# Later reciprocals, later queue issues and three more VectorE groups in a planned kernel of attention and a gated feed-forward part

## The chip, the cores and the metric

The kernel runs on one core of one Trainium2 chip. A core has five engines that run side by side, each through its own list of instructions in order: TensorE (PE, matrix products), ScalarE (ACT), VectorE (DVE), GpSimd (POOL) and SyncE (SP), which here only issues DMA transfers. TensorE writes to PSUM, eight banks of 128 x 512 fp32; the other data lie in SBUF. The metric is the device time of one execution in microseconds (us); several runs are given by their median.

## The reference

With x of 2048 x 512 (bfloat16), 32 heads of 16, and a hidden width of 1792:

```python
xn = _layernorm(x, axis=-1)
# A: attention
qkv = (xn @ wqkv).reshape(B, S, 3, H, Dh)          # q, k, v: 32 heads x 2048 x 16
scores = einsum("bhqd,bhkd->bhqk", q, k) * (Dh ** -0.5)
p = softmax(scores, axis=-1)
o = einsum("bhqk,bhkd->bhqd", p, v)
# B: gated feed-forward
gate, up = xn @ W_gate, xn @ W_up
h = gate * (gate > 0) * up
out = x + o.reshape(B, S, D) @ wo + h @ W_down
```

There are 32 x 2048 x 2048 exponentials, 134 million of them. They are the bulk of the elementwise work.

## The kernel before

**Tiling.** The queries are cut into four chunks of 512 (`c4`), the heads into four groups (`gg`) of eight, and each group into its even and odd heads (`ee`): 32 blocks of four heads, in that order. The keys of a block are 16 tiles of 128 (`kt`). For one block and one key tile the scores of four heads are four tiles of 128 x 512. They are turned into exponentials in one of two ways.

- *ScalarE's way.* Two units for a key tile (`p` = 0, 1), each of two heads: TensorE writes scores into two PSUM banks (`P_sc` holds two such pairs), ScalarE makes one `Exp` of 128 x 1024 into a ring of 16 buffers (line 1347), and TensorE multiplies the tile by the values once.
- *VectorE's way, a group* (`quad`). The scores go one head at a time into one of the four shared banks (`P_b`). VectorE evicts each with an added bias into a 16-bit integer whose bits, read as bfloat16, are a rough exponential (line 1300). Two more patterns are made by adding a constant to all of these integers: the first by GpSimd or VectorE, by the share `POOL1_SHARE`, the second always by GpSimd, each in two pieces (line 1316; on VectorE line 1320, one instruction). The last two groups have both on VectorE (`LASTD`). TensorE multiplies all three by the values and adds them up, three value products where the other way has one; together they approximate the exponential.

`QUADS` says how many key tiles of each of the 32 blocks go VectorE's way (149 of 512 in all, so 1024 - 2 x 149 = 726 units are ScalarE's), and `QOFF` and, in the last block, `LAST_QUADS` say at which tiles: `int((a + QOFF) * 16 / q)` for a = 0 ... q - 1.

**Matmul form.** A matmul uses 64 rows and 32 columns of the array. Four of them side by side fill a half, and the two halves run independently (`mode="half"`). Weights are loaded by separate instructions; a load is left out when the half already holds the same ones (`wkey`), as between the three value products of a group when they follow each other.

**Sums.** The value matrix has a column of ones, so the softmax sums come out as one row of each head's product. When a block's products are complete, `normalise` (from line 1168) evicts the accumulator into `o_sb` (L1178), copies the sums into `rsum` by a DMA spread over 128 partitions (L1194), has VectorE take 128 x 16 reciprocals (L1198), stores these in DRAM (L1199), loads them back broadcast (L1202), and has GpSimd multiply (L1210 or L1215); for odd heads four DMAs then pack the result (`pk`, L1219).

**Background.** Projections of queries, keys and values, and 56 feed-forward tiles (`glu`: two weight loads L980 and L981 into three buffers, two products, evictions L989 and L993) and 16 output row tiles (`out_rows`) run on TensorE and VectorE between the scores, at due times counted in ScalarE units. `K_LEAD`, `Q_LEAD`, `W_LEAD`, `V_AT` and `WREST` are leads or places in such units. A projected query goes through `qf` and eight small DMAs (L873) to its four masked copies.

**The planner.** All operations are put into a `Graph` with reads, writes, duration and priority. `Graph.run` simulates the engines and fixes the order of instructions on each; `Graph.emit` adds the semaphore waits. In `ready(o)` an operation may start at the planned end of what it reads, plus its `slack` where the producer is neither TensorE nor a DMA; after a DMA, `DMA_SLACK` = 1000 ns later, or at once where that DMA is marked urgent, as the sums' copies of the last blocks are. A buffer that is not yet given is taken from the moment when its last user ends. These times set the order alone; on the chip an engine waits for the semaphore, and whatever stands behind the waiting instruction on that engine or queue waits too. `slot_for` gives out the four shared banks: accumulators (`open`) hold a bank for a whole block, and the last block has two of them (`LAST2`), the second with `extra` set. `TOGETHER = 2` puts all three value products of a group behind the second pattern in the order. The two lines that the change touches in `ready` are

```python
at = max(at, d.end if d.eng == "PE" else d.end + ((0.0 if d.urgent else self.DMA_SLACK) if d.eng == "SP" else o.slack))
...
    at = max(at, b[0])
```

Of the kernel before, what the change touches and what calls it, by code (L numbers as in the profile page):

```python
# [32 lines left out]
PV_SLACK = 100  # L33
W_LEAD = 12
Q_LEAD = 36
K_LEAD = 28
QN, KN, GN, RN = 3, 2, 5, 10
ROW_AT = 16
XBANKS = (0, 1, 2, 3)
# [3 lines left out]
NRAW = 4  # L43
NPAT = 5
LEAD = 15
QOFF = 0.2
EARLY = ()
AHEAD = 10
POOL_SHARE = 1.0
POOL_PIECES = 2  # L50
POOL1_SHARE = 0.5
TOGETHER = 2
LAST2 = 1
LASTD = 2
TAIL_URGENT = 3
SC_ORDER = (0, 2, 1, 3)
P1_OFF = 0.0
LAST_QUADS = 0.8
SPLIT = 8
PVBANKS = (0, 1, 2, 3)  # L60
PV_EARLY = False
REC = 'DVE'
POOL_NS = 1980
QUADS = [0, 3, 4, 4, 5, 5, 5, 5, 5, 5, 5, 5, 5, 4, 5, 5, 5, 5, 5, 5, 5, 5, 5, 4, 5, 5, 5, 5, 5, 5, 5, 5]


LOG2E = 1.4426950408889634
# [5 lines left out]
TR_URGENT = (0, 1, 1, 1)  # L73
TR_AFTER = (None, 1, None, None)
DMA_TR = (2, 3)
WREST = 6
Z_AT = 20
MASK_ACT = (0, 2)
MASK_LATE = 4
PER_TILE = (0,)  # L80
V_AT = (4, 8, 14, 20)
EXP_SCALE = 1.0 / (128.0 * LOG2E)
NUP = 1
NHS = 20
# [36 lines left out]
class Graph:  # L121
# [16 lines left out]

    def __init__(self):
        self.ops = []  # L140
        self.fillers, self.nfill = [], 0
        self.units = {}

    def op(self, eng, dur, fn, reads=(), writes=(), prio=0.0, order=(), name="", stream=None, lat=None, after=None,
# [44 lines left out]
    def run(self):  # L189
# [18 lines left out]
        def slot_for(t):  # L208

            best, second = None, None  # L210
            for i in (t.allowed if t.allowed is not None else range(len(t.pool.cur))):
                c = t.pool.cur[i]
                if c is None:
                    at = 0.0
                else:
                    us = c.w + c.r
                    if not all(u.done for u in us):
                        continue
                    at = max(u.end for u in us)
                if best is None or at < best[0]:  # L220
                    best, second = (at, i), best
                elif second is None or at < second[0]:
                    second = (at, i)
            if t.pool.shared:
                held = any(c is not None and c.open > 0 for c in t.pool.cur)
                if t.extra:
                    if t.extra.slot is None:
                        return None
                elif t.open:
                    if held and not (self.EARLY and second is not None):  # L230
                        return None
                elif not held and len(t.allowed) > 3:
                    return second
            return best

# [4 lines left out]
        def ready(o):  # L240
            at = 0.0
            for d in o.deps:
                at = max(at, d.end if d.eng == "PE" else d.end + ((0.0 if d.urgent else self.DMA_SLACK) if d.eng == "SP" else o.slack))
            for d in o.order:
                at = max(at, d.start if d.eng == o.eng else d.end)
            for t in o.acq:
                if t.slot is not None:
                    continue
                b = slot_for(t)
                if b is None:  # L250
                    return None
                at = max(at, b[0])
            return at

        def pe_start(o, at):
# [10 lines left out]
        held = [None, None]  # L266
# [53 lines left out]
        while n < len(ops):  # L320
# [8 lines left out]
            if got_pe is not None and best[1] == "PE":  # L329
                at, o = got_pe  # L330
                kind = None
                for f in self.fillers:
                    t = f[0].cur[f[1]]
# [25 lines left out]
            at, e, o = best  # L359
# [208 lines left out]
def bass_parallel_sum__mha_block__glu_gated_reglu__prompt_kernel(  # L568
# [14 lines left out]
    with ExitStack() as es:  # L583
        def sb(name, shape, dt):
# [34 lines left out]
        rsum = sb("rsum", [128, 2, 16], FP32)  # L619
        rrec = sb("rrec", [128, 2, 16], FP32)  # L620
# [8 lines left out]
        G = Graph()  # L629
# [25 lines left out]
             reads=[t_pid], writes=[t_pid], prio=-890)  # L655
        for v in (0, 2, 1, 3):
            G.op("DVE", 100, lambda e, v=v: e.tensor_scalar(hmask[:, v:v + 1], pid[:, 0:1], 16.0 * v, QSCALE, op0=ALU.is_equal, op1=ALU.mult),
                 reads=[t_pid], writes=[t_masks[v]], prio=-889 + v)
# [4 lines left out]
             reads=[t_id], writes=[t_id], prio=-898)  # L663
# [8 lines left out]

        def dma(fn, kb, writes=(), reads=(), prio=0.0, stream=None, order=(), name="dma", after=None, joins=()):
            return G.op("SP", 500, fn, reads=reads, writes=writes, prio=prio, stream=stream or ("o", len(G.ops)),
                        lat=kb, order=order, name=name, after=after, joins=joins)

        x_src = x2.rearrange("(m p) d -> p m d", p=128)
        t_x = [Tile("x") for _ in range(NB)]
# [42 lines left out]
        for j in range(4):  # L721
            for ee in range(2):
                r0 = 32 * j + DH * ee
                dma(lambda e, r0=r0, ee=ee: e.dma_start(Wo_l[r0:r0 + DH, ee, :], A_wo[D - 128 + r0:D - 128 + r0 + DH, :]), 16,
                    reads=[t_woz], writes=[Tile()], prio=60, after=100)
# [178 lines left out]
        for n, bk in enumerate(blocks):  # L904
            q = QUADS[n]
# [30 lines left out]
        for bank, c, tk in ((1, slice(0, 128), t_k0), (2, slice(128, 512), t_k[(0, 0)])):  # L936
            t = Tile("prok", P_b, [bank])
# [230 lines left out]
        def normalise(c4, gg, ee, second):  # L1168
# [21 lines left out]
            par = n % 2  # L1190
# [4 lines left out]
            if REC == "POOL":  # L1195
                G.op("POOL", 3060, lambda e: e.tensor_tensor(rrec[:, par, :], rsum[:, par, :], minus[:], ALU.pow), reads=[ts, t_ones], writes=[trr], prio=pr - 60)
            else:
                G.op("DVE", 190, lambda e: e.reciprocal(rrec[:, par, :], rsum[:, par, :]), reads=[ts], writes=[trr], prio=-940, name="rec")  # L1198
            dma(lambda e: e.dma_start(rec_scr[n].rearrange("j (i q) -> (j i) q", q=16), rrec[:, par, :]), 8,  # L1199
                reads=[trr], writes=[tsc], prio=pr - 50, stream=("n2", n % 4))  # L1200
            last_rec[n] = (ts, trr)
# [25 lines left out]
        def pv_stream(key, kt, src, reads, u, prio):  # L1227

            key = part(key + (kt,))
            c4, gg, ee = key[:3]  # L1230
            if key not in pv_tile:

                two = blocks.index(key[:3]) >= len(blocks) - LAST2
                a = Tile("pv", P_b, PVBANKS)
                b = Tile("pv", P_b, PVBANKS) if two else a
                pv_tile[key] = a, b
                count = sum(kinds.get(k, 1) for k in keys if part(k) == key)
                pv_left[key] = ([0, count], [0, count]) if two else ([0, 2 * count],) * 2
                a.open, b.extra = pv_left[key][0][1], a if two else None
                b.open = pv_left[key][1][1]  # L1240
                pv_ops[key] = []
            for half in range(2):
                t, st = pv_tile[key][half], pv_left[key][half]
                rows = slice(64 * half, 64 * half + 64)

                def vs(j, rows=rows):
                    a = VW * (8 * gg + 2 * j + ee) - DH * ee
                    return v_flat[rows, kt, a:a + 32]

                def vload(e, half=half, vs=vs):  # L1250
                    for j in range(4):
                        e.ldweights(vs(j), tile_position=(64 * half, 32 * j))  # L1252

                def pv(e, half=half, vs=vs, rows=rows, t=t, st=st):
                    ins = None
                    for j in range(4):
                        ins = matmul_loaded(e, ps[32 * j:32 * j + 32, BANK[t.slot], :], vs(j), src[j](rows), st[0] == 0, st[0] == st[1] - 1, (64 * half, 32 * j))
                    st[0] += 1
                    return ins
                o = G.op("PE", 216, pv, reads=[t_vones, t_v[kt]] + reads, joins=[t], prio=prio, name="pv%d" % u, mode="half", half=half, bank=(t, 0), slack=PV_SLACK,  # L1260
                         load=vload, weights=[t_vones, t_v[kt]], wkey=("v", gg, ee, kt))
                pv_ops[key].append(o)
            if len(pv_ops[key]) == 2 * sum(kinds.get(k, 1) for k in keys if part(k) == key):
                normalise(*key)
# [130 lines left out]
```

## Time and profile before

| | us |
|---|---|
| median of 3 runs (lowest, highest) | 706.99 (705.41, 708.81) |
| the profiled execution's own time | 706.39 |
| its span, first to last instruction | 704.5 |
| TensorE busy | 685.5 (97%), 22209 matmuls |
| ScalarE busy | 677.2 (96%) |
| VectorE busy | 591.1 (84%) |
| GpSimd busy | 491.2 (70%) |
| mean granted clock of TensorE | 0.997 |

A profile row of a group of instructions reads: line, engine, operation, written tiles <- read tiles, shapes, count, then busy time in us and the mean of one in ns, and last the engine's idle time just before these instructions, with what ended most of it. Mean durations overlap: the sum of the means is more than the busy time. A row of waits reads: who waited for whom, us in total, times, longest. `SPq` is the queue of SyncE, whose waits are counted from its previous instruction. A row of the chain that ended last reads: start, length, what. A row of stretches gives the stretch, its length, and for each engine its busy time and number of instructions, then TensorE's granted clock, the DMA engines' busy share and GB/s. TensorE's busy time has modelled ends.

### The profile page before, as it was taken

What the parts mean: (1) busy time and instruction counts of PE and PEld (TensorE: products, weight loads), DVE (VectorE), ACT (ScalarE), POOL (GpSimd) and SP (SyncE); (2) the same over time, 40 slices, a digit from 0 to 9 for tenths busy, and PEclk for the clock granted to TensorE, in tenths of its full rate; (3) what the DMA queues carried; (4) which work ended last, traced back from release to release, by engine and by line L of the source; (5) the groups of instructions that cost most, each with busy time, mean ns of one, the idle gap of its engine ahead of it and who ended that gap; (6) DMA issues with size and microseconds to landing.
All of it is one profiled execution on the core that took longest, in us unless ns stands there. A gap on an engine that the chain in (4) does not pass through costs nothing.

```text
span 704.5 us, 45927 instructions
## 1 busy us (share of the span) xinstructions
PE 685.5 (97%) x22209; PEld 389.9 (55%) x20697; DVE 591.1 (84%) x990; ACT 677.2 (96%) x734; POOL 491.2 (70%) x496
## 2 busy tenths in 40 slices
PE   8999999999999999999999999999999999999996
PEld 4555656555554755555554675655554565556543
DVE  8948788798999778989798779889889777999864
ACT  6999999999999999999999999999999999999993
POOL 3234756687768987867788878679677867787850
PEclk9999999999999999999999999999999999999998
DMA  7422322243201122232201112222211122221011
GB/s 210 63 65 52 74 57 61 57 131 86 70 21 36 35 69 56 67 74 64 46 18 42 39 51 72 68 56 56 55 41 35 32 56 60 57 67 45 27 28 36
DMA packets 95031, 41.16 MB, mean 58 GB/s; under 512 B 77240, under 2 KB 90872, under 8 KB 94840
## 3 DMA queue, kind: packets, MB, share of 16 engines
q1 hardware_dynamic: 94840, 38.22, 21.5%
q8 instruction: 168, 2.75, 1.7%
q14 instruction: 23, 0.19, 0.1%
HBM read 31.06 MB, written 2.35 MB: 47 GB/s over the span
## 4 chain that ended last, share of the span: by engine, by line
PE 72%; ACT 19%; DVE 5%; DMA 2%; issue 1%; SPq 0%; POOL 0%; DVEq 0%
PE ps L116 71%; ACT ring L1347 19%; DVE qd L1300 2%; DMA rsum<-o_sb 2%; DVE stats L745 1%; DVE qd L1320 0%; DVE xn_sb L758 0%; DMA x_sb<-in_A_x_dram 0%; DVE kT L883 0%; DVE hT L993 0%; DVE o_sb L1178 0%; PE ps L1362 0%; DVE rrec L1198 0%; DVE up_sb L989 0%; DVE xnT L797 0%
## 5 line engine op out<-in xcount | busy, mean ns | idle before, releaser
L1347 ACT ACTIVATE ring<-ps 128x1024 bf16<-128x1024 f32 x726 | 672.1, 1095 | 8.8 <-PE ps L116 7.8
L1316 POOL TENSOR_TENSOR qd<-qd,shift 128x512 int32<-128x512 int32 x440 | 443.9, 1038 | 163.3 <-DVE qd L1320 72.2
L116 PE MATMUL ps<-qT,kT 64*32 64x512 bf16 x8192 | 466.8, 375 | 8.2 <-DVE hT L993 1.5
L1300 DVE TENSOR_SCALAR qd<-ps 128x512 int16<-128x512 f32 x596 | 392.0, 685 | 66.9 <-PE ps L116 61.2
L116 PE MATMUL ps<-qd,v_aug 64*32 64x512 bf16 x3576 | 281.8, 375 | 1.1 <-PE ps L116 0.5
L116 PE MATMUL ps<-ring,v_aug 64*32 64x512 bf16 x2904 | 250.7, 375 | 0.9 <-issue 0.4
L1280 PEld LDWEIGHTS <-kT 64*32 64x32 bf16 x8092 | 176.7, 92 | 121.0 <-issue 31.8
L1252 PEld LDWEIGHTS <-v_aug 64*32 64x32 bf16 x5068 | 125.5, 92 | 73.6 <-issue 19.7
L116 PE MATMUL ps<-xnT,wgs 64*32 64x512 bf16 x1792 | 140.0, 375 | 0.4 <-issue 0.3
L116 PE MATMUL ps<-xnT,wus 64*32 64x512 bf16 x1792 | 138.3, 375 | 0.0
L825 PEld LDWEIGHTS <-wgs 64*32 64x32 bf16 x1792 | 44.4, 92 | 25.8 <-issue 7.1
L825 PEld LDWEIGHTS <-wus 64*32 64x32 bf16 x1792 | 44.2, 92 | 25.9 <-issue 7.2
L825 PEld LDWEIGHTS <-hT 64*32 64x32 bf16 x1792 | 44.5, 92 | 25.1 <-issue 4.0
L1320 DVE TENSOR_SCALAR qd<-qd 128x2048 int16<-128x2048 int16 x78 | 55.1, 716 | 2.7 <-PE ps L116 2.1
L116 PE MATMUL ps<-Wd,hT 64*32 64x512 bf16 x768 | 56.7, 375 | 0.2
L116 PE MATMUL ps<-Wk,hT 64*32 64x512 bf16 x512 | 42.2, 375 | 0.0
L989 DVE COPY up_sb<-ps 128x512 f32<-128x512 f32 x56 | 38.3, 683 | 4.7 <-PE ps L116 4.6
L993 DVE SCALAR_TENSOR_TENSOR hT<-ps,up_sb 128x512 bf16<-128x512 f32 x56 | 38.1, 680 | 3.8 <-PE ps L116 3.5
L116 PE MATMUL ps<-Wv,hT 64*32 64x512 bf16 x512 | 41.2, 376 | 0.0
L116 PE MATMUL ps<-xnT,Wq 64*32 64x512 bf16 x480 | 38.4, 375 | 0.0
L116 PE MATMUL ps<-Wo_p,x_sb 64*32 64x512 bf16 x480 | 37.6, 376 | 0.0
L116 PE MATMUL ps<-xnT,Wk 64*32 64x512 bf16 x480 | 35.2, 375 | 0.1
(70 smaller groups left out, 261.6 us busy)
## 6 DMA issues: line engine op xcount, KB each, us to landing
rb<-rec_scr SPq DMA_DIRECT2D x31, 256.0 KB
wus<-in_B_W_up_dram SPq DMA_DIRECT2D x56, 128.0 KB, 2.8
wgs<-in_B_W_gate_dram SPq DMA_DIRECT2D x56, 128.0 KB, 3.1
xr_sb<-in_A_x_dram SPq DMA_DIRECT2D x16, 128.0 KB, 3.1
qT<-qf SPq DMA_DIRECT2D x120, 16.0 KB, 2.2
out_dram<-xn_sb SPq DMA_DIRECT2D x15, 128.0 KB, 1.9
x_sb<-in_A_x_dram SPq DMA_DIRECT2D x8, 128.0 KB, 2.5
x_sb<-oT SPq DMA_DIRECT2D x60, 16.0 KB, 2.3
```

The costliest lines, as they stand in the source:

```text
L116: return e.add_instruction(mybir.InstMatmult(name=e.bass.get_next_instruction_name(), engine=mybir.EngineType.PE, ins=[e.lower_ap(x), e.lo ...
L745: G.op("DVE", 580, lambda e, m=m: e.bn_stats(stats[:, m, :], xs(m)), reads=[t_xm[m]], writes=[t_st], prio=pr)
L825: e.ldweights(w()[rows, 32 * j:32 * j + 32], tile_position=(rows.start, 32 * j))
L989: G.op("DVE", 603, lambda e: e.tensor_copy(up_sb[:, tup.slot, :], bank_of(tu)), reads=[tu], writes=[tup], prio=-590)
L993: G.op("DVE", 603, lambda e: e.scalar_tensor_tensor(out=hT[:, th.slot, :], in0=bank_of(tg), scalar=0.0, in1=up_sb[:, tup.slot, :], op0=ALU ...
L1252: e.ldweights(vs(j), tile_position=(64 * half, 32 * j))
L1280: e.ldweights(ks(m), tile_position=(64 * half, 32 * m))
L1300: G.op("DVE", 601, lambda e, j=j, tx=tx: e.tensor_scalar(qd[:, tq.slot, 512 * j:512 * j + 512], ps[:, BANK[tx.slot], :], IBIAS[3], 0.0, op ...
L1316: G.op("POOL", POOL_NS / POOL_PIECES + 60, lambda e, x=x, n=n, c=slice(i * m, i * m + m): e.tensor_tensor(x().bitcast(I32)[:, c], raw().bi ...
L1320: G.op("DVE", 600, lambda e, n=n, x=x: e.tensor_scalar(x(), raw(), float(SHIFTS[n + 1]), None, op0=ALU.add), reads=[ti, tq], writes=[t], p ...
L1347: exp_ops[u] = G.op("ACT", 904, lambda e, tr=tr, k0=k0: e.activation(ring[:, tr.slot, :, :], ps[:, 4 * k0:4 * k0 + 2, :], ACTF.Exp, scale= ...
```

## The change

- `QUADS`: blocks 3, 13 and 23 have five groups instead of four, 152 in all. `QOFF` 0.2 to 0.3 and `LAST_QUADS` 0.8 to 0.9 shift the tiles that they take.
- `POOL1_SHARE` 0.5 to 0.6: a larger part of the first patterns is GpSimd's.
- `TOGETHER` 2 to 0: the value products of a group are no longer ordered behind its second pattern.
- `REC_SLACK`: a reciprocal is planned 3000 ns instead of 1000 ns after the expected landing of its sums.
- `SP_SLACK`: DMAs of the streams `wu`, `wg` (feed-forward weights), `xr` (residual input), `q` (query copies) and `pk` (packing) are planned 2000 ns after what they read from another engine than TensorE, and 2000 ns after their buffer comes free.
- `slot_for`: while a second accumulator waits for its bank, the other users of all four banks leave one free.
- `K_LEAD`, `WREST`, `V_AT`: key projections four units earlier, the rest of two weights' loads four units earlier, value projections of the later key tiles later.

```diff
-K_LEAD = 28
+K_LEAD = 32
...
-QOFF = 0.2
+QOFF = 0.3
...
-POOL1_SHARE = 0.5
-TOGETHER = 2
+POOL1_SHARE = 0.6
+TOGETHER = 0
 LAST2 = 1
 LASTD = 2
+REC_SLACK = 3000
+SP_SLACK = 2000
...
-LAST_QUADS = 0.8
+LAST_QUADS = 0.9
...
-QUADS = [0, 3, 4, 4, 5, 5, 5, 5, 5, 5, 5, 5, 5, 4, 5, 5, 5, 5, 5, 5, 5, 5, 5, 4, 5, 5, 5, 5, 5, 5, 5, 5]
+QUADS = [0, 3, 4, 5, 5, 5, 5, 5, 5, 5, 5, 5, 5, 5, 5, 5, 5, 5, 5, 5, 5, 5, 5, 5, 5, 5, 5, 5, 5, 5, 5, 5]
...
-WREST = 6
+WREST = 2
...
-V_AT = (4, 8, 14, 20)
+V_AT = (4, 10, 18, 26)
...
-                elif not held and len(t.allowed) > 3:
+                elif len(t.allowed) > 3 and (not held or any(b.slot is None and b.extra.slot is not None for b in self.twins)):
                     return second
...
-                at = max(at, d.end if d.eng == "PE" else d.end + ((0.0 if d.urgent else self.DMA_SLACK) if d.eng == "SP" else o.slack))
+                at = max(at, d.end if d.eng == "PE" else d.end + ((0.0 if d.urgent else max(self.DMA_SLACK, o.slack)) if d.eng == "SP" else o.slack))
...
-                at = max(at, b[0])
+                at = max(at, b[0] + (o.slack if o.eng == "SP" else 0.0))
...
         def dma(fn, kb, writes=(), reads=(), prio=0.0, stream=None, order=(), name="dma", after=None, joins=()):
             return G.op("SP", 500, fn, reads=reads, writes=writes, prio=prio, stream=stream or ("o", len(G.ops)),
-                        lat=kb, order=order, name=name, after=after, joins=joins)
+                        lat=kb, order=order, name=name, after=after, joins=joins,
+                        slack=SP_SLACK if stream and stream[0] in ("wu", "wg", "xr", "q", "pk") else 0.0)
...
-                G.op("DVE", 190, lambda e: e.reciprocal(rrec[:, par, :], rsum[:, par, :]), reads=[ts], writes=[trr], prio=-940, name="rec")
+                G.op("DVE", 190, lambda e: e.reciprocal(rrec[:, par, :], rsum[:, par, :]), reads=[ts], writes=[trr], prio=-940, name="rec", slack=REC_SLACK)
...
-                a.open, b.extra = pv_left[key][0][1], a if two else None
+                a.open = pv_left[key][0][1]
+                if two:
+                    b.extra = a
+                    G.twins.append(b)
```

More of the change, by code (lines that the diff above doesn't have):

```diff
@@ L140, in __init__ @@
         self.ops = []
-        self.fillers, self.nfill = [], 0
+        self.fillers, self.nfill, self.twins = [], 0, []
         self.units = {}
```

## The prediction

> **What bounds the kernel now.** I read the page's busy times first, then its groups of instructions, then the waits of every engine, the chain that ended last, and last the busy times of chosen stretches.
>
> ```profile
> span 704.5 us, 45927 instructions
> ...
> PE 685.5 (97%) x22209; PEld 389.9 (55%) x20697; DVE 591.1 (84%) x990; ACT 677.2 (96%) x734; POOL 491.2 (70%) x496
> ...
> L1347 ACT ACTIVATE ring<-ps 128x1024 bf16<-128x1024 f32 x726 | 672.1, 1095 | 8.8 <-PE ps L116 7.8
> L1300 DVE TENSOR_SCALAR qd<-ps 128x512 int16<-128x512 f32 x596 | 392.0, 685 | 66.9 <-PE ps L116 61.2
> L1320 DVE TENSOR_SCALAR qd<-qd 128x2048 int16<-128x2048 int16 x78 | 55.1, 716 | 2.7 <-PE ps L116 2.1
> ```
>
> The reader is to see that ScalarE's exponentials (L1347) are the bound. The 726 of them take 672.1 us with their overlaps taken out, 0.926 us each, and ScalarE sat idle before them for only 8.8 us. They run from 11.9 us to about 692.8 us; the 12 us ahead and behind are start and finish. TensorE's 97% says less, for matmul ends are modelled. A better figure comes from its densest stretch, below: 580 matmuls in 16 us, that is 72.5 rounds of eight (four column tiles in each of two row halves), so a round takes at most 0.221 us. 22209 matmuls are then about 613 us, 89% of the 690 us in which they run. TensorE has a little room, VectorE (84%) some, GpSimd more.
>
> Next, who waits:
>
> ```profile
> DVE rrec L1198 <- DMA rsum<-o_sb: 8.8, 8, 2.3
> ACT ring L1347 <- PE ps L116: 7.8, 17, 1.6
> PE ps L116 <- DVE qd L1300: 1.4, 3, 1.1
> ...
> SPq L980 <- PE ps L116: 101.9, 38, 6.7
> ```
>
> VectorE stood eight times, 8.8 us in all, at a reciprocal whose sums had not landed, with every eviction behind it. The chain that ended last runs through the largest of these:
>
> ```profile
> 345.16 0.66 SPq L980
> 345.82 0.04 issue
> 345.86 0.51 SPq L981
> 346.37 0.04 issue
> 346.42 2.04 DMA rsum<-o_sb
> 348.46 0.02 issue
> 348.48 0.25 DVE rrec L1198
> ...
> 350.56 31.32 ACT ring L1347 x34
> ```
>
> Here the copy of the sums was not slow (2.04 us); it was issued late, because the queue of SyncE stood at a weight load (L980) whose buffer TensorE had not given back. The evicted sums had been ready at 343.2 us. The stretches show the price and the room:
>
> ```profile
> core 0: us, PE busy (x) PEld busy (x) DVE busy (x) ACT busy (x) POOL busy (x), PEclk, DMA share, GB/s
> 138.00:146.00 8.00, 6.94 (x217) 3.48 (x192) 6.78 (x13) 7.27 (x9) 7.42 (x9) 1.00 0.54 141
> 304.00:312.00 8.00, 7.48 (x260) 3.82 (x232) 5.54 (x10) 7.57 (x9) 2.88 (x4) 1.00 0.36 79
> 346.00:354.00 8.00, 6.49 (x220) 3.51 (x196) 5.17 (x10) 6.45 (x8) 5.28 (x6) 1.00 0.39 95
> 596.00:604.00 8.00, 6.87 (x236) 3.75 (x213) 5.79 (x11) 6.61 (x8) 4.58 (x5) 1.00 0.31 82
> 560.00:576.00 16.00, 15.80 (x580) 10.26 (x540) 12.48 (x20) 15.81 (x18) 10.30 (x11) 1.00 0.13 36
> 88.00:110.00 22.00, 21.91 (x740) 11.70 (x696) 18.28 (x31) 21.98 (x25) 12.73 (x13) 1.00 0.26 62
> 299.00:321.00 22.00, 21.48 (x724) 11.73 (x660) 17.42 (x28) 21.57 (x24) 14.74 (x15) 1.00 0.30 72
> 506.00:528.00 22.00, 21.84 (x716) 12.88 (x664) 19.33 (x32) 21.98 (x25) 16.25 (x16) 1.00 0.15 38
> ```
>
> In the first four, the stretches behind the reciprocals that waited 1.0 to 2.3 us, ScalarE is idle for 0.73 + 0.43 + 1.55 + 1.39 = 4.1 us: nearly half of all its idle time. The other four waits (0.4 to 0.6 us) left no gap there.
>
> **The change part by part.**
>
> Three more groups (blocks 3, 13 and 23 from four to five). Each takes two exponentials off ScalarE: 6 x 0.926 = 5.55 us less, on the bound. Each gives TensorE three value products in place of one, so 3 x 2 x 0.221 = +1.3 us, beside ScalarE's work where TensorE has room. VectorE gets 12 evictions at 392.0/596 = 0.658 us, +7.9 us. With the share of first patterns on GpSimd going from half to 0.6, VectorE makes 64 of them instead of 78: 14 x 55.1/78 = -9.9 us, so -2.0 us net. GpSimd makes 40 pieces more at 443.9/440 = 1.009 us, +40 us: 76% of the span, hidden. But a block with five groups has 22 exponentials instead of 24, 20.4 us. The last three rows are these blocks (their exponentials start at 89.0, 297.7 and 505.1 us): VectorE has 18.3, 17.4 and 19.3 us of work in each and gains four evictions, 2.6 us: 20.9, 20.0 and 21.9 us into 20.4. About 0.5, 0 and 1.5 us do not fit and have to go to the neighbours. Bounds of this cost on ScalarE: nothing (VectorE as a whole is idle for a sixth of the span) and the 5.55 us gained. I take the 0.5 + 1.5 = 2.0 us, as if none could move, nearer the first bound, since the other evictions are due evenly along the span.
>
> The move of patterns onto GpSimd is where a rule speaks against the change. The row is that L1316 on GpSimd waited 72.2 us for L1320 on VectorE, while L1320 itself waited 2.7 us: GpSimd pays, VectorE does not. The Trainium skill (Perfetto Trace Analysis, Optimizing Scalar/DVE Operations) warns that the two share an SBUF port and that shifting work between them might not help. If VectorE got no relief from it, each of the three blocks would keep 2.5 patterns instead of 2 on it, 3 x 0.5 x 0.706 = 1.1 us, an estimate, and the time would be that much higher; the trace, with 2.7 us against 72.2, does not bear it out.
>
> Reciprocals later. The planner puts each at the landing it expects plus 3.0 us instead of 1.0, hence 2.0 us further back among the evictions. The waits of 1.0, 1.6, 1.9 and 2.3 us shrink to 0, 0, 0 and 0.3, so about 4.1 us of ScalarE's idle time goes. The last two sums are marked urgent and keep their place (0.55 us at 679.7, without a gap on ScalarE). What is late next: the store of the reciprocals and their broadcast, queued on SyncE behind it, and GpSimd's multiplication. Before, the multiplication starts 7 to 11 us after the reciprocal and its rows wait 10.9 + 2.5 us in seven places, 8.2 of it at the very end where nothing else is due; 2 us are covered by that distance. Were they not, GpSimd stands 2 us and the patterns behind it are late, at most 2 us in a block. I take nothing.
>
> Queue issues behind their buffers. Weight, residual, query and packing transfers are planned 2.0 us after the release. This puts the sums' copy ahead of L980 and L873 in SyncE's order, a second cure of the same 4.1 us, not a second gain. Its price: weights land up to 2 us later. From the issue plus 2.8 us to landing (the page's median), the weights of 53 of the 56 feed-forward tiles have 6 us or more until their first load, and the three others 1.3, 3.1 and 4.8 us (306 to 317 and 520 us). Bounds: nothing and 0.7 us; I take nothing, as the queue no longer stands there.
>
> Value products no longer held back until the second pattern: TensorE may take a group's first product as soon as four evictions are done. Nearest rows: TensorE waited 1.4 us for these evictions. Bounds: -1 us (a smoother TensorE) and the rival below; I take nothing. Weight sharing may suffer. Of 2904 + 3576 value matmuls, 5068 loads remain, 1412 are shared; if all sharing goes, 353 rounds of four loads come back. In the stretch of 560 to 576 us, 135 such rounds of loads lie under 580 matmuls, and 145 rounds of matmuls on two halves left no visible room between them. So a load is hidden, and I take nothing. The Trainium skill (TensorE: Matmul & The Clock Gate, The mechanism) says that a load overlaps matmuls in flight only when the row group differs; then each would cost its own half the mean duration of a load at L1252, 353 x 0.092 / 2 = 16 us, an estimate; the stretch just named speaks against it.
>
> The rest. In a block of five one group moves from tile 3 to tile 4: nothing, its lead of ten exponentials stays. In the last block the last group goes from tile 10 to 12, leaving six exponentials (5.6 us) after it against 4 x 0.685 + 2 x 0.716 = 4.2 us on VectorE; between -1 and +1 us, I take nothing. Later value projections (2 to 6 exponentials) are covered by the ring of 16 exponentials, 14.8 us; uncovered, up to 5.6 us once. Key projections come 3.7 us sooner, into stretches at 546 to 548 of 580 matmuls. The rest of two weights is already issued at 7.7 us behind the inputs; nothing. The bank kept for the last block's second accumulator touches 20 us alone; nothing.
>
> The sum: 704.5 - 5.55 - 4.1 + 2.0 = 696.9 us of span, with the 1.9 us around it 698.7 us against the profiled 706.39. That execution is 0.6 us under the median of the runs, so 699.3 us by the median: 1.1% faster. A measurement of this kernel can tell about 0.5% (3.5 us) from no change.
>
> **The rivals.**
> - One of the two gains is lost. Either the three blocks become TensorE's and VectorE's (for: 21.9 us of work in 20.4 in the third; against: 16% idle VectorE over the span), or the wait of the reciprocals comes back elsewhere, in SyncE's order (for: SyncE stands 55.9 us at the stores of the reciprocals, L1199). Then 706.99 - 4.1 = 702.9 or 706.99 - 5.55 + 2.0 = 703.4: call it 703.
> - More than forecast: TensorE's freer order takes also the other 4.7 us of ScalarE's idle time, 694 to 695 us.
> - Slower, by the freed value products. TensorE runs in order; if a group's first product stands directly behind its evictions, any lateness of VectorE stops the scores behind it and so ScalarE. Now such products stand behind the patterns, a microsecond or two later, and lateness is hidden. For: VectorE is busy 15.2 of every 16 us from 176 to 224 us. Against: 61.2 us of VectorE's waits are for TensorE, the other way round. There are 152 groups; with 0.12 us each it is 18 us, 717 us. It decides from (7.7 + 3.5) / 152 = 74 ns a group.
> - Weight loads that come back cost TensorE time. With all 353 rounds unhidden, 0.092 us each on one of two halves, it is 16 us: 715 us. The stretch at 580 matmuls speaks against it.
>
> **How the numbers follow.** Forecast 0.50 (its own range 695 to 703), one gain lost 0.24 (half of it under 703.5), more gain 0.04, slower by freed products 0.20 (a seventh of it milder, within the bound), loads 0.02. Faster: 0.48 + 0.12 + 0.04 = 0.64; same: 0.02 + 0.12 + 0.03 = 0.17; slower: 0.19. The range of 8 in 10 goes from 693, all idle time gone, to 711, half of the slower case.
>
> **What would show it.** Right: 720 exponentials, busy near 667 us; waits of L1198 for the sums under 1 us in all; idle before L1347 at 5 to 7 us; sums issued before L980 where they were behind. Wrong: TensorE waiting for L1300 by many microseconds (freed products); exponentials with a mean over 0.93 us (TensorE the bound); VectorE over 97% around 90 and 510 us with ScalarE's gaps there; a higher count of loads at L1252 with fewer matmuls per stretch.

## The result

| | us |
|---|---|
| kernel before, median of 17 runs (lowest, highest) | 708.38 (704.89, 711.38) |
| changed kernel, median of 17 runs | 702.76 (700.42, 706.30) |
| ratio, 95% interval | 0.9931 (0.9911 to 0.9951) |
| profiled execution of the changed kernel, its span | 705.23, 703.4 |

The kernel became 0.69% faster, about 5 us; 699.3 us had been forecast, with 693 to 711 as the range. The two profiled executions show less than that: the one of before is 2.0 us faster than its median, the one of the changed kernel 2.5 us slower than its own. So their spans differ by 1.1 us only, and what is read below are rows and not the difference of the spans. Totals of idle time share this: they belong to one execution each.

The page of the changed kernel (busy times, then groups of instructions with count, busy us, mean ns, idle before them):

```profile
span 703.4 us, 46489 instructions
...
PE 681.9 (97%) x22255; PEld 385.0 (55%) x21161; DVE 591.4 (84%) x988; ACT 672.1 (96%) x728; POOL 531.0 (75%) x536
...
L1353 ACT ACTIVATE ring<-ps 128x1024 bf16<-128x1024 f32 x720 | 667.1, 1085 | 12.7 <-PE ps L118 11.1
...
L1306 DVE TENSOR_SCALAR qd<-ps 128x512 int16<-128x512 f32 x608 | 400.6, 686 | 77.5 <-PE ps L118 72.3
...
L1326 DVE TENSOR_SCALAR qd<-qd 128x2048 int16<-128x2048 int16 x64 | 45.7, 720 | 0.8 <-PE ps L118 0.5
```

The counts are those worked out (720, 608, 64; GpSimd at 531 us), and ScalarE's exponentials take 5.0 us less. But ScalarE idles 12.7 us before them in this execution, instead of 8.8. The rise of 3.9 us is no larger than the 4.5 us by which the two executions lie off their medians, and the changed kernel's profile in e5 has 8.3 us. So the rows show that the work left; whether the time went with it is a matter for the experiments.

The waits (who for whom, us in total, times, longest), with SyncE's own at the end:

```profile
ACT ring L1353 <- PE ps L118: 11.1, 24, 1.1
...
PE ps L118 <- issue: 5.6, 14, 0.9
...
PE ps L118 <- POOL qd L1322: 1.6, 2, 1.0
...
DVE rrec L1201 <- DMA rsum<-o_sb: 0.2, 1, 0.2
```

```profile
SPq L983 <- PE ps L118: 69.1, 34, 5.1
```

VectorE's 8.8 us of waiting for sums are 0.2. ScalarE's waits are now many and short: 24, none over 1.1 us, where there were 17 of up to 1.6 us. TensorE stands 5.6 us at "issue", where it waits for nothing that the profile shows (2.1 us before). SyncE's queue stands 69.1 us for the weights' buffers instead of 101.9. The stretches that answer to those shown of before are the four behind the old waits, and the three blocks that got a fifth group:

```profile
core 0: us, PE busy (x) PEld busy (x) DVE busy (x) ACT busy (x) POOL busy (x), PEclk, DMA share, GB/s
138.00:146.00 8.00, 8.00 (x276) 4.33 (x264) 7.35 (x13) 8.00 (x10) 6.55 (x7) 1.00 0.29 76
304.00:312.00 8.00, 8.00 (x273) 5.12 (x252) 7.45 (x14) 8.00 (x10) 5.97 (x7) 1.00 0.22 50
346.00:354.00 8.00, 7.51 (x256) 3.88 (x236) 6.48 (x12) 7.34 (x9) 5.53 (x6) 1.00 0.36 79
596.00:604.00 8.00, 7.86 (x282) 4.02 (x258) 6.32 (x11) 7.42 (x9) 5.38 (x6) 1.00 0.16 45
89.00:109.00 20.00, 20.00 (x708) 11.19 (x663) 17.87 (x30) 20.00 (x23) 15.19 (x16) 1.00 0.24 59
297.00:317.00 20.00, 20.00 (x682) 11.98 (x640) 18.01 (x30) 19.69 (x22) 17.05 (x18) 1.00 0.23 54
506.00:526.00 20.00, 20.00 (x688) 13.26 (x648) 19.19 (x33) 20.00 (x24) 16.79 (x18) 1.00 0.16 40
```

ScalarE's 4.1 us of gaps in the first four are 1.2 us, and what remains there is not at a reciprocal. In the last three ScalarE is full or nearly so (19.69 of 20 us in the second) and VectorE is not: the 2.0 us that the forecast set aside for these blocks were not paid.

### The profile page after: what moved, and what is told of

It is laid out like the page before. It is cut to its first block, busy times and chain, and to the rows that moved or that the text cites. A ratio compares the mean times of both kernels' runs of the same rounds, so it can differ in the third digit from the quotient of the medians.

```text
span 703.4 us, 46489 instructions
## 1 busy us (share of the span) xinstructions
PE 681.9 (97%) x22255; PEld 385.0 (55%) x21161; DVE 591.4 (84%) x988; ACT 672.1 (96%) x728; POOL 531.0 (75%) x536
## 4 chain that ended last, share of the span: by engine, by line
PE 78%; ACT 15%; DVE 3%; issue 2%; POOL 1%; DMA 0%; ACTq 0%; DVEq 0%; POOLq 0%
PE ps L118 77%; ACT ring L1353 15%; DVE qd L1306 1%; POOL qd L1322 1%; DVE stats L748 1%; DVE xn_sb L761 0%; DMA x_sb<-in_A_x_dram 0%; DVE xn_sb L1034 0%; DVE hT L996 0%; POOL x_sb L1213 0%; PE ps L1368 0%; DVE xnT L800 0%; PE ps L821 0%; DVE xn_sb L1147 0%; PE ps L1124 0%
## 5 line engine op out<-in xcount | busy, mean ns | idle before, releaser
L1353 ACT ACTIVATE ring<-ps 128x1024 bf16<-128x1024 f32 x720 | 667.1, 1085 | 12.7 <-PE ps L118 11.1
L1322 POOL TENSOR_TENSOR qd<-qd,shift 128x512 int32<-128x512 int32 x480 | 483.5, 1041 | 120.7 <-DVE qd L1326 66.1
L1306 DVE TENSOR_SCALAR qd<-ps 128x512 int16<-128x512 f32 x608 | 400.6, 686 | 77.5 <-PE ps L118 72.3
L118 PE MATMUL ps<-qd,v_aug 64*32 64x512 bf16 x3648 | 301.2, 375 | 3.4 <-POOL qd L1322 1.6
L118 PE MATMUL ps<-ring,v_aug 64*32 64x512 bf16 x2880 | 256.1, 375 | 1.9 <-issue 0.9
L1286 PEld LDWEIGHTS <-kT 64*32 64x32 bf16 x8092 | 174.9, 92 | 124.2 <-issue 32.6
L1258 PEld LDWEIGHTS <-v_aug 64*32 64x32 bf16 x5532 | 135.9, 92 | 77.9 <-issue 21.1
L118 PE MATMUL ps<-xnT,wgs 64*32 64x512 bf16 x1792 | 137.3, 375 | 0.3 <-issue 0.3
L118 PE MATMUL ps<-Wd,hT 64*32 64x512 bf16 x768 | 54.6, 375 | 0.3 <-DVE qd L1306 0.3
L1326 DVE TENSOR_SCALAR qd<-qd 128x2048 int16<-128x2048 int16 x64 | 45.7, 720 | 0.8 <-PE ps L118 0.5
```

The costliest lines, as they stand in the source:

```text
L118: return e.add_instruction(mybir.InstMatmult(name=e.bass.get_next_instruction_name(), engine=mybir.EngineType.PE, ins=[e.lower_ap(x), e.lo ...
L1286: e.ldweights(ks(m), tile_position=(64 * half, 32 * m))
L1306: G.op("DVE", 601, lambda e, j=j, tx=tx: e.tensor_scalar(qd[:, tq.slot, 512 * j:512 * j + 512], ps[:, BANK[tx.slot], :], IBIAS[3], 0.0, op ...
L1322: G.op("POOL", POOL_NS / POOL_PIECES + 60, lambda e, x=x, n=n, c=slice(i * m, i * m + m): e.tensor_tensor(x().bitcast(I32)[:, c], raw().bi ...
L1326: G.op("DVE", 600, lambda e, n=n, x=x: e.tensor_scalar(x(), raw(), float(SHIFTS[n + 1]), None, op0=ALU.add), reads=[ti, tq], writes=[t], p ...
L1353: exp_ops[u] = G.op("ACT", 904, lambda e, tr=tr, k0=k0: e.activation(ring[:, tr.slot, :, :], ps[:, 4 * k0:4 * k0 + 2, :], ACTF.Exp, scale= ...
```

## The experiments

Two gains were claimed: 4.1 us from the waits and 5.55 us from six exponentials less, the second on the ground that ScalarE is the bound. The rival was that one of the two is lost. All ratios are to the kernel before on the same chip. e1 to e8 ran on one chip and e9 to e12 on another, where the kernel before takes 701 to 702 us; a ratio can be compared across them, a time or a profile's total less well.

### e5: the changed kernel on that chip

> The changed kernel as it is, beside the kernel before on the chip on which the variants are compared, so that undoing a part can be held against it. Expected: ratio 0.991 to 0.995 to the kernel before. If the chip mattered and not the schedule, the ratio would be another, 0.998 to 1.002; then the variants' ratios of e1 to e3 would read otherwise.

No edit. Measured: 696.12 us to 702.24, ratio 0.9903 (0.9874 to 0.9932). The gain is there on this chip too, and is not smaller than on the first. ScalarE idles 8.3 us here, TensorE's issue gaps are 3.6 us.

### e6: the waits alone, in the same order

```diff
-                G.op("DVE", 190, lambda e: e.reciprocal(rrec[:, par, :], rsum[:, par, :]), reads=[ts], writes=[trr], prio=-940, name="rec")
+                G.op("DVE", 190, lambda e: e.reciprocal(rrec[:, par, :], minus[:]), reads=[ts, t_ones], writes=[trr], prio=-940, name="rec")
...
         G.run()
+        for o in G.ops:
+            if o.name == "rec":
+                o.deps = {d: True for d in o.deps if d.eng != "SP" or d.stream[0] != "n1"}
```

> The kernel before with the same order on every engine, in which the 31 reciprocals read a constant instead of the sums and so wait for no DMA; the softmax is then not normalised, that part of the result is left out. It prices the wait alone, without a new plan. Theory of the prediction: VectorE's 8.8 us of waiting go, 4.1 us of ScalarE's idle time go, and the time falls by 3 to 4.5 us: ratio 0.994 to 0.996. Rival (the work behind catches up, the wait costs nothing): ratio 0.998 to 1.001.

Measured: 696.36 us, ratio 0.9921 (0.9892 to 0.9950), 5.5 us of 702 (3.5 to 7.6). The wait has a price; the expected 0.994 to 0.996 lies at the upper end of the interval. The groups of this kernel:

```profile
L1347 ACT ACTIVATE ring<-ps 128x1024 bf16<-128x1024 f32 x726 | 668.0, 1120 | 2.7 <-PE ps L116 2.0
L1198 DVE RECIPROCAL rrec<-minus 128x16 f32<-128x16 f32 x31 | 7.5, 242 | 0.0
```

The kernel before, in its old order with 149 groups and 726 exponentials, is as fast as the changed one (696.12 us) once VectorE doesn't stand at the sums. The last reciprocals wait for nothing here either, but the finish does not make the gain: from the last exponential's end at 682.7 us to the end of the span at 694.3 it takes 11.6 us, 11.7 in the profile of before. ScalarE's idle time is 2.7 us, 6.1 below the profile of before. That is more than the 4.1 us counted in the four gaps, but the profile of before was taken on another chip, so what the rest is owed to is not shown.

### e7: six exponentials alone, in the same order

```diff
-            exp_ops[u] = G.op("ACT", 904, lambda e, tr=tr, k0=k0: e.activation(ring[:, tr.slot, :, :], ps[:, 4 * k0:4 * k0 + 2, :], ACTF.Exp, scale=EXP_SCALE),
+            exp_ops[u] = G.op("ACT", 904, lambda e, tr=tr, k0=k0, n=32 if blocks.index(key[:3]) in (3, 13, 23) and key[3] == 6 else 512: e.activation(ring[:, tr.slot, :, 0:n], ps[:, 4 * k0:4 * k0 + 2, 0:n], ACTF.Exp, scale=EXP_SCALE),
```

> The kernel before with the same order on every engine, in which six exponentials (tile 6 of blocks 3, 13 and 23, both units) make 64 elements a partition instead of 1024; the rest of these two tiles' exponentials is left out. It prices the six exponentials on ScalarE alone. Theory (ScalarE is the bound): 6 x 0.65 to 0.75 us = 3.9 to 4.5 us less, ratio 0.993 to 0.996. Rival (TensorE is the bound, ScalarE only waits longer for scores): ratio 0.998 to 1.001, ScalarE's idle time up by 3 us or more.

Measured: 701.44 us, ratio 0.9988 (0.9962 to 1.0014). The rival's ratio came, not the theory's. ScalarE's idle time, 9.1 us, can't be held against the rival's 3 us or more, for want of a profile of the kernel before on this chip. The six short ones take 0.29 us each. What happens behind two of the three pairs can be seen in ScalarE's order of time (start, length, what, count, idle before):

```profile
92.25 4.03 ACT L1347 ACTIVATE ring<-ps 128x1024 bf16<-128x1024 f32 x5
96.74 0.22 ACT L1347 ACTIVATE ring<-ps 128x64 bf16<-128x64 f32 x1 [0.45 <-PE ps L116]
98.49 1.94 ACT L1347 ACTIVATE ring<-ps 128x1024 bf16<-128x1024 f32 x2 [1.53 <-PE ps L116]
...
505.29 3.15 ACT L1347 ACTIVATE ring<-ps 128x1024 bf16<-128x1024 f32 x4
508.98 0.22 ACT L1347 ACTIVATE ring<-ps 128x64 bf16<-128x64 f32 x1 [0.53 <-PE ps L116]
509.84 4.95 ACT L1347 ACTIVATE ring<-ps 128x1024 bf16<-128x1024 f32 x5 [0.64 <-PE ps L116]
```

ScalarE saves 1.3 us on a pair and waits 1.2 to 2.0 us for the next scores right behind it. At the first of these, and at the pair not shown (302 us), VectorE stood 1.0 and 2.0 us at a reciprocal just then, which hides what the pair alone would do. The last is nearly free of that (0.29 us), and there TensorE is full by its modelled busy time (its 164 matmuls are about 90% of what the densest stretch of before makes in 5 us):

```profile
507.00:512.00 5.00, 4.99 (x164) 2.52 (x140) 4.71 (x9) 3.81 (x7) 3.51 (x5) 1.00 0.19 44
```

So in this order ScalarE, given less to do, only waits for TensorE's scores. Whether TensorE's own rate or the order of its instructions holds them back is not shown. Where the order is laid anew, as in the change, this run doesn't say what the groups are worth.

### e1: the slacks alone, with a new order

```diff
# the kernel before, with the bank rule of e10
-                at = max(at, d.end if d.eng == "PE" else d.end + ((0.0 if d.urgent else self.DMA_SLACK) if d.eng == "SP" else o.slack))
+                at = max(at, d.end if d.eng == "PE" else d.end + ((0.0 if d.urgent else max(self.DMA_SLACK, o.slack)) if d.eng == "SP" else o.slack))
...
-                at = max(at, b[0])
+                at = max(at, b[0] + (o.slack if o.eng == "SP" else 0.0))
...
-                        lat=kb, order=order, name=name, after=after, joins=joins)
+                        lat=kb, order=order, name=name, after=after, joins=joins,
+                        slack=2000 if stream and stream[0] in ("wu", "wg", "xr", "q", "pk") else 0.0)
...
-                G.op("DVE", 190, lambda e: e.reciprocal(rrec[:, par, :], rsum[:, par, :]), reads=[ts], writes=[trr], prio=-940, name="rec")
+                G.op("DVE", 190, lambda e: e.reciprocal(rrec[:, par, :], rsum[:, par, :]), reads=[ts], writes=[trr], prio=-940, name="rec", slack=3000)
```

> The kernel before with the two slacks alone (reciprocals at the expected landing + 3.0 us, the five DMA streams + 2.0 us) and the bank rule for the last block, 149 groups as before. Theory (two gains, 5.55 us of exponentials and 4.1 us of reciprocal waits, some of it given back): waits of the reciprocals under 1 us, ScalarE's idle time 4 to 6 us lower unless new gaps take its place, time 704 against 708.4, ratio 0.992 to 0.996. Rival (the slacks only trade one wait for another, the gain is the exponentials'): waits gone, but ratio 0.998 to 1.002. Rival (the slacks are the whole gain): 0.991 to 0.994 and ScalarE idle under 6 us.

Measured: 705.02 us, ratio 1.0043 (1.0025 to 1.0061). The reciprocals wait 0.0 us and ScalarE idles 5.3 us, as the theory says, and yet the time rose. In the profile the last exponential ends at 687.2 us, but the span at 701.9: 14.7 us of finish, 11.7 in the kernel before. None of the three expectations holds as stated: the wait went, and the time did not. The longer finish is a part of it only: against e6, on the same chip and also without these waits, the last exponential ends 4.5 us later and the finish takes 3.1 us more. So taking the wait away is worth its price in the old order (e6), and not in every order.

### e10: the bank rule alone

```diff
-                elif not held and len(t.allowed) > 3:
+                elif len(t.allowed) > 3 and (not held or any(b.slot is None and b.extra.slot is not None for b in self.twins)):
```

> The kernel before with the bank rule of the last block alone. e1 had this rule and both slacks, no waits of reciprocals, and was yet 0.4% slower than the kernel before; its last 15 us after the exponentials were 3 us longer than before. Theory (the rule alone delays the end of the last block, which hid the gain of the slacks in e1): ratio 1.003 to 1.009, the time after the last exponential 13 to 15 us against 11.7 before. Rival (the rule costs nothing, the slacks lose what they win elsewhere): ratio 0.998 to 1.002.

Measured: 702.77 us, ratio 1.0020 (1.0003 to 1.0037), with 12.1 us of finish in the profile: the rival's numbers, at their upper end. The rule alone costs at most 0.4%, and little of that at the end, so e1's 3 us more of finish come from the slacks' new order or from both together. The rule is not a part that can be left out: neither the groups nor the reciprocals' slack could be put into the old order without it, for the planner found no bank for the last block's second accumulator.

### e2 and e3: the groups added alone, and undone alone

```diff
# e2: the kernel before, with the bank rule
-QUADS = [0, 3, 4, 4, 5, 5, 5, 5, 5, 5, 5, 5, 5, 4, 5, 5, 5, 5, 5, 5, 5, 5, 5, 4, 5, 5, 5, 5, 5, 5, 5, 5]
+QUADS = [0, 3, 4, 5, 5, 5, 5, 5, 5, 5, 5, 5, 5, 5, 5, 5, 5, 5, 5, 5, 5, 5, 5, 5, 5, 5, 5, 5, 5, 5, 5, 5]
# e3: the changed kernel, with this line the other way round
```

> The kernel before with 152 groups in place of 149 and the bank rule for the last block; the reciprocals and the queue stay as they were. Theory: 720 exponentials at 0.926 us, 5.5 us less busy ScalarE, the reciprocal waits near 9 us as before; time 703 to 705, ratio 0.992 to 0.996. Rival (three blocks are bound by TensorE and VectorE, so the exponentials taken off only become idle time): ScalarE idle 13 us or more, ratio 0.998 to 1.003.

> The changed kernel with the 149 groups of before, all else kept. Theory: loses the exponentials' 5.5 us, keeps the removed waits: 705 to 708, ratio 0.996 to 1.000. Rival (the exponentials were hidden, the gain is the waits'): as the changed kernel, ratio 0.992 to 0.994.

Measured: e2 713.76 us, ratio 1.0157 (1.0131 to 1.0182); e3 709.20 us, ratio 1.0097 (1.0067 to 1.0126). Both are far slower than either theory allows, in opposite edits. Their profiles show where some of it is lost. First e2's groups, its TensorE (scores, then a value product) and ScalarE's longest gap:

```profile
L1350 ACT ACTIVATE ring<-ps 128x1024 bf16<-128x1024 f32 x720 | 666.0, 1089 | 21.9 <-PE ps L116 20.9
```

```profile
480.11 0.38 PE L116 MATMUL ps<-qT,kT 64*32 64x512 bf16 x8
...
484.00 0.38 PE L116 MATMUL ps<-ring,v_aug 64*32 64x512 bf16 x4
```

```profile
484.48 1.94 ACT L1350 ACTIVATE ring<-ps 128x1024 bf16<-128x1024 f32 x2 [4.42 <-PE ps L116]
```

The 720 exponentials cost 666.0 us, as counted, and 21.9 us of idle time come with them. For 4.4 of these TensorE was busy (8.00 of 8 us from 478 to 486) with other products. The scores were there by 480.5 us; the exponential stood for one of the 16 buffers of the ring, and started when TensorE ended the value product of 484.0 us that gave it back (the semaphore it waits for is that product's). e3 has a hole of 4.0 us at 196.7 us, at a block's second exponential, and this one is a late query projection:

```profile
194.37 2.62 SPq L876 DMA_DIRECT2D qT<-qf  x3
```

```profile
200.77 4.69 ACT L1353 ACTIVATE ring<-ps 128x1024 bf16<-128x1024 f32 x5 [4.04 <-PE ps L118]
```

The block's eight query copies are issued from 189.8 to 197.0 us (182.9 to 189.4 before), the last lands at 199.4, and ScalarE goes on at 200.8. So a new constant moves a value product or a query projection by some microseconds in the planner's order, and a hole opens or closes there. What the groups themselves are worth can't be read from these two runs.

### e9 and e11: the slacks undone, and the products held back again

```diff
# e9
-REC_SLACK = 3000
-SP_SLACK = 2000
+REC_SLACK = 1000
+SP_SLACK = 0
# e11
-TOGETHER = 0
+TOGETHER = 2
```

> The changed kernel with both slacks undone (reciprocals at the expected landing + 1.0 us, the five DMA streams without slack), all else kept. Theory after e6 (the removed wait is nearly the whole gain): the reciprocals wait again, 5 to 9 us in all, and the time goes up by 4 to 6 us against the changed kernel: ratio 0.996 to 1.000 to the kernel before. Rival (the other constants carry the gain): ratio 0.989 to 0.992.

> The changed kernel with the value products of a group held behind its second pattern again. Theory of the prediction (this edit costs and brings nothing by itself): ratio 0.988 to 0.994, within 2 us of the changed kernel; the loads at L1258 fall from 5532 to about 5100. Rival (the freedom is needed for 152 groups, as e2 with 152 groups and held products was 1.6% slower): ratio 0.998 to 1.012, ScalarE's idle time over 15 us.

Measured: e9 710.11 us, ratio 1.0122 (1.0092 to 1.0151); e11 701.81 us, ratio 1.0009 (0.9995 to 1.0024). e9's waits came back as expected,

```profile
DVE rrec L1201 <- DMA rsum<-o_sb: 11.2, 9, 2.7
```

but the loss of some 2% against the changed kernel is more than this, and beyond both expectations; its finish takes 18.8 us (last exponential 689.4, span 708.2). e11, whose ratio is in the rival's range though ScalarE's idle time is 6.6 us and not over 15, gives the plainest case of that. Its value loads fall to 4992 as foreseen, its TensorE's issue gaps are 1.2 us, and its last exponential ends at 681.1 us, 4.1 us sooner than in e5's profile of the changed kernel. Its finish then takes 18.8 us:

```profile
681.00:690.00 9.00, 6.76 (x172) 2.62 (x116) 8.15 (x15) 0.11 (x1) 1.27 (x1) 1.00 0.03 11
690.00:700.00 10.00, 4.17 (x67) 1.95 (x66) 3.63 (x9) 0.00 (x0) 0.00 (x0) 0.70 0.17 54
```

Five evictions and four patterns of the last groups stand on VectorE after ScalarE is done (681 to 688 us), and the last products wait for them. The changed kernel has two such patterns, done at 690.6, before its last exponential. So this order, with the products held back, is not neutral as forecast, but what it loses it loses at the end of the plan, and not through TensorE's waits or through the loads.

### e4, e8 and e12: what the weight transfers cost

```diff
# e4 in the changed kernel, e8 in the kernel before; wgs alike
-            dma(lambda e: e.dma_start(wus[:, tw.slot, :, :], wu_src), 128, writes=[tw1], joins=[tw], prio=pr - W_LEAD, stream=("wu", k % (2 * NWS)), after=pr - W_LEAD)
+            dma(lambda e: e.dma_start(wus[:, tw.slot, :, :], wu_src) if k < NWS else e.dma_start(wus[0:1, tw.slot, 0, :], wu_src[0:1, 0, :]), 128, writes=[tw1], joins=[tw], prio=pr - W_LEAD, stream=("wu", k % (2 * NWS)), after=pr - W_LEAD)
# e12 in the changed kernel; behind each weight load of the first query chunk in SyncE's order, for up and gate:
+dma(lambda e, scr=scr, src=src, ft=ft: e.dma_start(scr[ft].rearrange("p dt f -> p dt f"), src), 128, stream=("ws", n, ft % 2))
-            dma(lambda e: e.dma_start(wus[:, tw.slot, :, :], wu_src), 128, writes=[tw1], joins=[tw], prio=pr - W_LEAD, stream=("wu", k % (2 * NWS)), after=pr - W_LEAD)
+            dma(lambda e: e.dma_start(wus[:, tw.slot, :, :], wu_src if c4 == 0 else wu_scr[ft]), 128, writes=[tw1], joins=[tw], prio=pr - W_LEAD, stream=("wu", k % (2 * NWS)), after=pr - W_LEAD)
```

> The changed kernel with the same plan, but from the fourth feed-forward tile on each of the two weight loads moves one row of 256 bytes instead of 128 KB; the feed-forward products then use stale weights, so this part of the result is left out. In the changed kernel TensorE stood 14 times, 5.6 us, waiting for nothing that the profile shows, each time about 1 us behind a 16 KB packet of the instruction queue that had started late. Theory (TensorE's instruction packets queue behind the data transfers and come late): with 14 MB less in 57000 packets, these gaps fall under 2 us, ScalarE's idle time falls by 4 us or more, and the time is 2 to 5 us under the changed kernel's 702.8: 698 to 701, ratio 0.985 to 0.990. Rival (the gaps come from the instruction stream itself, not from other transfers): gaps still 4 to 6 us, ratio 0.991 to 0.995.

> The kernel before with the same plan and the weight loads cut to 256 bytes from the fourth feed-forward tile on (stale weights; the feed-forward part of the result is left out). Theory (late instruction packets cost both kernels, and the changed one only a little more): ratio 0.988 to 0.993, TensorE's waits for nothing from 2.1 to under 1.2 us, the reciprocal waits still several us. Then the changed kernel's plan, freed of the packets' lateness, is 4 to 8 us shorter than this one. Rival (the changed plan alone suffers from the transfers): ratio 0.997 to 1.001.

> The changed kernel with the same order on all engines but SyncE's queue, where 28 transfers are added in the first query chunk: each copies one feed-forward weight tile in DRAM into a layout in which a later load moves 128 packets of 1 KB instead of 512 of 256 bytes; the loads of the other three chunks use the copies. Theory (late instruction packets wait behind the many small packets): TensorE's waits for nothing fall under 2.5 us, the time by 1 to 2.5 us against the changed kernel: ratio 0.986 to 0.989. Rival (the bytes count, not the packets, or the copies cost as much as they save): ratio 0.990 to 0.993.

Measured: e4 692.58 us, ratio 0.9864 (0.9841 to 0.9887); e8 698.37 us, 0.9946 (0.9927 to 0.9965); e12 699.28 us, 0.9970 (0.9950 to 0.9991). e4 came as its theory said, in ratio and gaps; e8 gained less than its theory and more than its rival. e4's rows:

```profile
L1353 ACT ACTIVATE ring<-ps 128x1024 bf16<-128x1024 f32 x720 | 662.7, 1107 | 3.4 <-PE ps L118 2.8
```

```profile
PE ps L118 <- issue: 1.2, 3, 0.6
```

The transfers of the weights cost both kernels nearly the same: 696.12 - 692.58 = 3.5 us the changed one, 702.24 - 698.37 = 3.9 us the one before. So TensorE's issue gaps, which are longer in the changed kernel's profiles (5.6 and 3.6 us against 2.1), are not what keeps the change from a larger gain: freed of the transfers the change is worth 1 - 0.9864/0.9946 = 0.8%, about what it is with them (0.97% on this chip).

How the transfers reach TensorE stays open. In the trace one 16 KB packet of the instruction queue goes with about every 256 TensorE instructions, and each of the ten issue gaps over 0.2 us between 30 and 690 us of the changed kernel's profile begins 0.4 to 1.4 us behind a packet's landing, though packets come only every 4 us. But the packets that start late, over 300 instructions after the one before, are 12 in the changed kernel and 13 in e4, where the gaps are nearly gone. And packing the weights into a quarter of the packets, e12, left 4.5 us of issue gaps and brought no gain over the changed kernel (0.9970 against 0.9903 and 0.9931): neither the theory's number nor the rival's.

## Why the prediction was right, and where it was not

**Direction and range.** Faster, 702.8 us in 693 to 711 and in the forecast's own 695 to 703. The size was 1.1% forecast and 0.69% measured (0.49 to 0.89). That it came so near is partly luck: the gain put down to the exponentials was not seen, the cost put down to crowding was not paid, and the two errors are of opposite sign.

**The reciprocals' wait (-4.1 us): right.** The wait went from 8.8 to 0.2 us, and alone, in an unchanged order, it is worth 5.5 us (e6), with the forecast's 4.1 inside the interval of 3.5 to 7.6. The row of the profile that carried it was the chain through L980, the sums' copy and the reciprocal. What was put at nothing behind it stayed so: GpSimd's multiplications wait 9.5 + 1.3 us for the broadcast, 10.9 + 2.5 before. The forecast assumed that the gain survives a new order, and e1 shows an order in which it does not.

**The six exponentials (-5.55 us): this step failed.** It was put as "on the bound". Busy time fell by about as much as worked out (672.1 to 667.1), but the idle time of 5 to 7 us that was to go with it did not come: 12.7 us, and 8.3 in e5. e7 shows that ScalarE, given less to do in a fixed order, waits for TensorE within two exponentials: 0.8 us gained, with an interval that reaches from a gain of 2.7 to a loss of 1.0. A 96% busy engine with 8.8 us of idle time was taken for the bound by itself, and TensorE, which has to deliver its scores, for an engine with room, on an average of 89% over the span. The rival "one of the two gains is lost" comes nearest to this, and its price of 703 us (0.6%) to what was measured. Open is whether the groups bring something in the new order that another of the constants takes away: e5 against e6, the whole change against the waits alone, differ by 0.2%, less than either's interval of 0.3% to each side.

**Crowding in the three blocks (+2.0 us): not paid.** ScalarE is full in the first and third and 0.3 us idle in the second, with VectorE at 89 to 96%. The forecast put the VectorE work of 22 us, and 2.6 us more, into blocks of 20.4 us; a shorter block also has less of the other work, and 20 us of the changed kernel hold 17.9, 18.0 and 19.2 us of it.

**Queue issues behind their buffers (0): not told apart from the reciprocals' slack.** Only both together were undone (e9). In the changed kernel's trace three sums' copies are still issued 1.1 to 3.4 us after the eviction, eight by 1.8 to 3.3 us before, so the queue's order did improve; the reciprocals, mostly seven to ten VectorE instructions behind the eviction in place of five, no longer meet the rest.

**Value products no longer held (0, rival slower with 0.20): wrong in sign and place.** TensorE's waits for these evictions are 1.1 us, as short as before (1.4), so the slower rival has no support (TensorE waits 1.6 us for GpSimd's patterns, which it did not name). But planned anew with held products the kernel loses a percent (e11 against the changed kernel), at the end of the plan. The forecast had looked at the middle of the plan alone. Of the loads: 5532 instead of 5068 at L1258, with no stretch that shows them; the issue of loads on TensorE did not become the bound.

**The other constants (0 each): not tested one by one.** In sum they and the groups net to nothing that can be told from noise: the waits alone give 0.9921, the whole change 0.9903 on the same chip.

## What to carry to other kernels

Where a planner fixes the order, price a part by an edit that keeps the order: take the wait away, or shorten the instruction, and leave the plan alone. Undoing one constant and planning anew moved the time by 1 to 2%, largely through holes and finishes elsewhere in the plan. And before work taken off the busiest engine is counted in full, shorten a few of its instructions in the old order, and see whether the engine that feeds it can keep up. Look at the finish separately: the time after the last exponential ran from 11.6 to 18.8 us among orders of nearly the same work.

## What the runs showed of the hardware that was not expected

TensorE's granted clock fell in the finish, by very different amounts: to 0.70 in e11's last 10 us, with 4.17 us of TensorE busy, but only to 0.97 in the changed kernel's, with 4.47 us:

```profile
693.00:703.00 10.00, 4.47 (x112) 2.46 (x92) 4.46 (x11) 0.00 (x0) 0.00 (x0) 0.97 0.17 54
```

From 690 to 700 us e1 has 0.67 with 5.29 us busy and e9 0.82 with 8.39 us busy, so the busy share of the stretch alone does not decide it, and what does is not shown. Over the whole time after the last exponential the clock is 0.71 in e1 and 0.68 in e9, but 0.84 in e11 and 0.85 in the kernel before. So the longer finishes of e1 and e9 are in part ones at a lower clock; how much of their length that makes is not shown either. The 32 small products that spread the last reciprocals (L1132) lie there: one takes 375 ns on average in e11 and 276 ns in the changed kernel. And cutting 14 MB of weight transfers, for which no instruction of TensorE waits in the profiles of before, of the changed kernel or of e5, made both kernels 3.5 to 3.9 us shorter.
